# MoE 2 with experts 1 to 7 in falling order of their token counts, and with 480 to 352 rows by place in that order

## The chip, the core and the metric

The kernel runs on one core of a Trainium2 chip. The metric is the device time of one execution in microseconds (us); smaller is better. Its engines are TensorE (PE, with PEld for its weight loads), VectorE (DVE), ScalarE (ACT), GpSimd (POOL) and SyncE (SP). Here SP only issues DMA transfers; POOL issues the indirect ones. Each engine works through its own instructions in a fixed order.

## The reference

A linear-attention layer and a first mixture block ("MoE 1") give `x` with N = 3072 tokens of D = 384. The change concerns what follows, the second mixture ("MoE 2"), where each token goes to the one expert of eight with the largest logit:

```
logits = x @ w_gate                      # 3072 x 8
expert_idx = np.argmax(logits, axis=1)
...
for e in range(E):                       # E = 8, F = 1024
    mask = expert_idx == e
    xe = x[mask]
    h = np.maximum(xe @ w1[e], 0.0)      # 384 -> 1024
    ye = h @ w2[e]                       # 1024 -> 384
    out[mask] = gate_w[mask, None] * ye
```

So the work per expert depends on how many tokens chose it, which is known only when the last token has been routed. Worked out from the reference's own inputs, expert 0 has 426 tokens, and experts 1 to 7 have, sorted, 469, 416, 410, 390, 361, 322 and 278.

## The kernel before

Attention fills about the first half of the time; MoE 1 then runs over six blocks of 512 tokens, from about 550 to 846 us. After each block `route` finds every token's expert and its rank within it, and POOL scatters the token's row (384 values, its gate weight, its number) into the DRAM table `slots`, which has 512 places (`CAP`) for each expert. A token beyond place 512 is left to a loop at the end (`For_i`, line 1519), which runs no turn when every count is at most 512.

MoE 2 takes expert after expert, 0 to 7, always with all 512 places, filled or not. Products keep float32 accuracy by splitting each operand into a high and a low part (H, L), so each product is three matmuls. `load_expert` issues four weight DMAs of 768 KB on SP into buffers `r` (pool `wr`, four buffers) and then makes the split weights: ACT copies the high part (line 249: six of 128x512 into `a1H`, eight of 128x384 into `a2H`), and POOL subtracts for the low part (line 250). Two pools, `wwa` and `wwb`, hold split weights of alternate experts. `load_rows` loads an expert's rows from `slots` in tiles of 128 (line 1199), `load_xt` transposes them on PE (`pxe`, line 1208) and splits them with ACT and DVE (`yTH`, `yTL`, lines 1209 and 1210).

`unit` computes one expert. For each of eight slices f of the 1024 hidden values, the first layer is nine matmuls into `ph` (line 1234; the moving operand is the rows, so its columns are the rows' number). ACT and DVE make `hH` and `hL` of it (1237, 1238). The second layer (lines 1222 to 1224, `pz`) is three matmuls for each tile of up to 128 rows: there the rows are the stationary operand, and the 384 columns of the weights move. The second layer of slice f runs behind the first layer of slice f + 1. At the end of a unit the next expert's transposes go in front of the last slice's second layer; then ACT scales each tile (`yo`, 1254) and POOL scatters it to the output (1255).

Expert 0 is done in two halves: its first 256 rows run (`half1`) while the last block is still being routed, with `gH`, `gL` in place of `hH`, `hL`, in pools of MoE 1; the other 256 rows follow in `expert_pass`. Buffers of `expert_pass` lie where MoE 1's buffers were, so its first row load waits for the last readers of those. The order of instructions on each engine is decided when the kernel is built. Before `expert_pass`, PE sums the counts (`pcn`, line 1474), DVE forms the number of extra turns `nx_`, and SP reads it into a register (line 1516).

Of the kernel before, what the change touches and what calls it, by code (L numbers as in the profile page):

```python
# [7 lines left out]
FP32 = mybir.dt.float32  # L8
# [3 lines left out]
I32 = mybir.dt.int32  # L12
# [168 lines left out]
def kernel(ctx: ExitStack, tc: tile.TileContext, q, k, v, beta, w_in, w_out, w_gate, w1, w2, out):  # L181
# [977 lines left out]
    def bank(name):  # L1159
        return ps.tile([128, 512], FP32, tag="ps", name=name)  # L1160

    wr = ahead["wr"]
    wwa = ctx.enter_context(tc.tile_pool(name="wwa", bufs=1, reuse_waits="tile"))

# [7 lines left out]

    def load_expert(e, wpool):
        r1, r2 = [], []
        for x in range(2):
            t_ = wr.tile([128, KD, F2 // 2], FP32, tag="rst", name="r1")
            load(e, out=t_, in_=w1[e].rearrange("(c p) f -> p c f", p=128)[:, :, x * F2 // 2:(x + 1) * F2 // 2])
            r1.append(t_)
        for x in range(2):
            t_ = wr.tile([128, KF2 // 2, DM], FP32, tag="rst", name="r2")  # L1180
            load(e, out=t_, in_=w2[e].rearrange("(c p) f -> p c f", p=128)[:, x * KF2 // 2:(x + 1) * KF2 // 2])
# [12 lines left out]

    def load_rows(e, sl, tiles, rpool, tag, bufs=2):
        rw = []
        for t in tiles:
            r_ = rpool.tile([128, RW], FP32, tag=tag, name="rw", bufs=bufs)
            last_rows[:] = [nc.sync.dma_start(out=r_, in_=sl[e * CAP + t * 128:e * CAP + (t + 1) * 128]).ins]
            rw.append(r_)  # L1200
        return rw

    def load_xt(rw, xt):
        n = len(rw) * 128
        for c in range(KD):
            p_ = bank("pxe")[:, 0:n]
            for t, r_ in enumerate(rw):
                pe.transpose(p_[:, t * 128:(t + 1) * 128], r_[:, c * 128:(c + 1) * 128], ident)
            act.activation(xt[0][:, c, 0:n], p_, ACTF.Copy)
            dve.tensor_tensor(xt[1][:, c, 0:n], p_, xt[0][:, c, 0:n].bitcast(FP32), ALU.subtract)  # L1210
        return xt

    def unit(ws, rw, xt, hpool, tags, ytag, between=None, final=False):

        a1, a2 = ws
        n, nt = 128 * len(rw), len(rw)
        py = [bank(f"pz{t}") for t in range(nt)]

        def second(fp, hh, hl, t):
            ts_ = slice(t * 128, (t + 1) * 128)  # L1220
# [31 lines left out]
        for t in range(nt):  # L1252
            yo = ytag[0].tile([128, 512], FP32, tag=ytag[1], name="yo", bufs=ytag[2])[:, 0:DM]
# [13 lines left out]

    pre = load_expert(0, wwa)
    with mx:
# [16 lines left out]
        eb = wp.tile([128, E], FP32, name="eb")  # L1286
        dve.tensor_copy(eb, ebi)
        tidi = wp.tile([128, 4], I32, name="tidi")
        for hb in range(2):
# [125 lines left out]
        for b in range(NT // 512):  # L1415
# [7 lines left out]
            for f in range(NF2 + SK):  # L1423
# [31 lines left out]
                if b == NT // 512 - 1:  # L1455
                    if f == SK + 1:
                        pad_first()
                    if f == SK + 4:
                        first["rows"] = load_rows(0, slots, range(2), rp, "row2")
                    if f == NF2 - 1:  # L1460
                        first["xt"] = load_xt(first["rows"], x_tiles(b + 1))
# [4 lines left out]
        step(last, 1)  # L1466
        half1 = unit(step(pre, 99), first["rows"], first["xt"], gp, ("gH", "gL", SK + 1), (gp, "t", 2))
        step(half1, 3)
        step(last, 1)
        step(half1, 2)  # L1470

        pk = bank("pcn")
        for n, x in enumerate(counts):
            pe.matmul(pk[:, 0:E], oneb, x, start=n == 0, stop=n == len(counts) - 1)
        mc = const.tile([128, 1], FP32, name="mc")
        dve.tensor_reduce(mc, pk[:, 0:E], AX.X, ALU.max)
        mci = const.tile([128, 1], I32, name="mci")
        dve.tensor_scalar(mci, mc, -1.0, None, ALU.add)
        nx_ = const.tile([128, 1], I32, name="nx_")
# [4 lines left out]
    wwb = ctx.enter_context(tc.tile_pool(name="wwb", bufs=1, reuse_waits="tile"))  # L1484
    hp = ctx.enter_context(tc.tile_pool(name="hp", bufs=3, reuse_waits="tile"))
# [4 lines left out]

    def expert_pass(sl, ws, t0):

        rw = load_rows(0, sl, range(t0, CAP // 128), yp, "rw", 8)
        xt = load_xt(rw, new_xt())
        for e in range(E):
            nx = load_expert(e + 1, (wwb, wwa)[e % 2]) if e + 1 < E else None
            nxt = []
            if nx:
                step(nx, 1)
                nrw = load_rows(e + 1, sl, range(CAP // 128), yp, "rw", 8)  # L1500
            run = unit(ws, rw, xt, hp, ("hH", "hL", 3), (yp, "yo", 4), (lambda: nxt.extend(load_xt(nrw, new_xt()))) if nx else None, final=not nx)
# [7 lines left out]
            if nx:  # L1509
                ws = step(nx, 99)  # L1510
                rw, xt = nrw, nxt

    expert_pass(slots, step(pre, 99), FIRST // 128)


    extra = nc.values_load(nx_[0:1, 0:1], min_val=0, max_val=NT // CAP)
    off = const.tile([128, 1], FP32, name="off")
    dve.memset(off, 0.0)
    with tc.For_i(0, extra, 1):
        dve.tensor_scalar(off, off, float(CAP), None, ALU.add)  # L1520
        clear_slots()
        for i in range(NT // 128):
# [43 lines left out]
```

## Time and profile before

| | |
|---|---|
| median of 3 runs | 1159.25 us (1151.38 to 1160.28) |
| the profiled execution | 1153.81 us, span 1152.1 us |
| busy, whole span | PE 938.5 us (81%), DVE 641.1, ACT 639.1, POOL 451.5 |
| expert 0's first half begins on PE | 846.16 us |
| its second half begins (first transpose) | 869.36 us |
| last second-layer matmul of expert 7 begins | 1136.13 us |

The busy shares are means over stages of different kind; MoE 2 is a stage of its own and is read from its own stretch. On PE consecutive matmuls overlap, so the distance between starts tells what one costs, not its printed duration. "Idle before, releaser" at the end of a timeline row is how long the engine had waited and for what.

### The profile page before, as it was taken

To read this page: it belongs to the slowest core of one execution; us is meant where nothing else is said; L and a number is where in the kernel's file an instruction comes from. 1 tells how busy PE (TensorE), PEld (TensorE's weight loads), DVE (VectorE), ACT (ScalarE), POOL (GpSimd) and SP (SyncE) were. 2 spreads that over 40 slices of the span, in tenths; PEclk is the share of its full clock that TensorE was granted. 3 is DMA by queue.
4 is the path that set the end of the run, shared out by engine and by line. 5 is a ranking of instruction groups with operands and counts; after the bars stand their busy time and mean duration, and the time that the engine had idled before them with its cause. 6 is when DMAs were issued, how large, how long until landed. Compare 5 with 4: busy or idle time off the path is not lost.

```text
span 1152.1 us, 23064 instructions
## 1 busy us (share of the span) xinstructions
PE 938.5 (81%) x9149; PEld 857.7 (74%) x9149; DVE 641.1 (56%) x1548; ACT 639.1 (55%) x1258; POOL 451.5 (39%) x451
## 2 busy tenths in 40 slices
PE   1222687688766788889899999999997999999994
PEld 0212587577656777787789988989896999999994
DVE  6778877978858959664875454444341222221220
ACT  4565899788797796785673333333324344432321
POOL 4453363554444723433432031210115665445611
PEclk9999999798778998889899999999998999999997
DMA  7976487594794975554654123230217543334100
GB/s 179 207 165 112 60 157 143 129 166 90 169 150 112 193 150 134 131 166 153 223 162 139 56 84 104 54 121 1 98 57 251 170 128 116 114 124 143 52 26 25
DMA packets 258727, 144.45 MB, mean 125 GB/s; under 512 B 200221, under 2 KB 241217, under 8 KB 258608
## 3 DMA queue, kind: packets, MB, share of 16 engines
q1 hardware_dynamic: 250480, 124.67, 45.9%
q0 software_dynamic: 7584, 17.41, 4.7%
q8 instruction: 73, 1.20, 0.4%
q10 hardware_dynamic: 544, 0.80, 0.2%
q14 instruction: 46, 0.38, 0.1%
HBM read 77.41 MB, written 36.60 MB: 99 GB/s over the span
## 4 chain that ended last, share of the span: by engine, by line
PE 43%; DVE 21%; issue 14%; ACT 10%; DMA 5%; POOL 4%; SPq 1%; POOLq 0%; ACTq 0%; DVEq 0%
PE ph L1234 9%; PE ph L1436 7%; DVE sub L35 3%; DVE Xp L35 3%; PE pz L1222 3%; PE pz L1224 3%; PE pz L1223 3%; PE ph L35 3%; DVE nw L35 3%; PE py L35 2%; PE py L1451 2%; PE py L1452 2%; PE py L1450 2%; ACT W L35 2%; DVE uL L35 1%
## 5 line engine op out<-in xcount | busy, mean ns | idle before, releaser
L1238 DVE SCALAR_TENSOR_TENSOR hL<-ph,hH 128x512 fp32r<-128x512 f32 (+1 forms) x64 | 42.0, 658 | 191.9 <-ACT hH L1237 191.9
L1237 ACT ACTIVATE hH<-ph 128x512 fp32r<-128x512 f32 (+1 forms) x64 | 36.8, 577 | 132.7 <-PE ph L1234 132.6
L1439 ACT ACTIVATE t<-ph,half 128x512 f32<-128x512 f32 x66 | 45.4, 688 | 93.7 <-PE ph L1436 93.2
L1440 DVE SCALAR_TENSOR_TENSOR t<-t,ph 128x512 f32<-128x512 f32 x66 | 45.2, 686 | 87.2 <-ACT t L1439 87.0
L1255 POOL DMA_INDIRECT out_dram<-yo,rw x32 | 31.3, 977 | 134.8 <-ACT yo L1254 129.9
L1222 PE MATMUL pz<-a2H,hH 128*128 128x384 f32 x240 | 81.9, 341 | 2.5 <-ACT hH L1237 2.5
L35 POOL TENSOR_TENSOR Pst<-pm,Pst 64x512 f16<-64x512 f32 x48 | 56.4, 1175 | 64.1 <-ACT Pst L35 63.0
L1224 PE MATMUL pz<-a2H,hL 128*128 128x384 f32 x240 | 81.4, 339 | 0.0
L1223 PE MATMUL pz<-a2L,hH 128*128 128x384 f32 x240 | 81.0, 338 | 0.0
L1396 POOL DMA_INDIRECT slots<-row,di x24 | 23.9, 997 | 144.7 <-DVE di L1388 139.2
L35 POOL TENSOR_TENSOR gL<-t,gH 128x256 fp32r<-128x256 f32 x60 | 46.5, 775 | 85.5 <-ACT gH L35 82.5
L1444 DVE TENSOR_TENSOR gL<-t,gH 128x512 fp32r<-128x512 f32 x66 | 54.6, 827 | 39.6 <-ACT gH L1443 38.8
L1234 PE MATMUL ph<-yTH,a1L 128*128 128x512 f32 (+1 forms) x192 | 73.5, 383 | 0.0
L1234 PE MATMUL ph<-yTL,a1H 128*128 128x512 f32 (+1 forms) x192 | 73.4, 382 | 0.0
L1234 PE MATMUL ph<-yTH,a1H 128*128 128x512 f32 (+1 forms) x192 | 72.7, 380 | 0.0
L35 PE MATMUL ph<-xTH,wiH 128*128 128x256 f32 x180 | 59.5, 330 | 12.6 <-DVE t L35 7.8
L1443 ACT ACTIVATE gH<-t 128x512 fp32r<-128x512 f32 x66 | 41.6, 631 | 47.7 <-DVE t L1440 47.7
L1450 PE MATMUL py<-woH,gH 128*128 128x392 f32 x192 | 65.6, 342 | 0.8 <-ACT gH L1443 0.8
L1451 PE MATMUL py<-woL,gH 128*128 128x392 f32 x192 | 65.3, 340 | 0.0
L1452 PE MATMUL py<-woH,gL 128*128 128x392 f32 x192 | 65.3, 340 | 0.0
L35 DVE TENSOR_TENSOR Xp<-Xp,sub 128x31 f32<-128x31 f32 (+15 forms) x186 | 63.7, 343 | 2.6
L35 DVE TENSOR_TENSOR sub<-Bt,Xp 128x31 f32<-128x31 f32 (+15 forms) x186 | 61.7, 332 | 4.9 <-POOL Bt L35 1.5
(306 smaller groups left out, 3261.0 us busy)
## 6 DMA issues: line engine op xcount, KB each, us to landing
r<-in_moe_w_dram SPq DMA_DIRECT2D x32, 768.0 KB, 4.5
slots<-zrow SPq DMA_DIRECT2D x8, 784.0 KB, 5.6
rw<-slots SPq DMA_DIRECT2D x32, 196.0 KB, 2.5
stage<-in_moe_w_in_dram SPq DMA_DIRECT2D x16, 384.0 KB, 3.7
stage<-in_moe_w_out_dram SPq DMA_DIRECT2D x16, 384.0 KB, 3.9
row<-ypart SPq DMA_DIRECT2D x6, 784.0 KB, 4.5
ysave<-row SPq DMA_DIRECT2D x6, 784.0 KB, 3.6
kr<-in_k_dram SPq DMA_DIRECT2D x24, 192.0 KB, 4.7
```

Of the source, the lines that this page charges most:

```text
L35: return self.fn(*self.a, **self.k)
L1222: pe.matmul(o, hh[:, ts_], a2[0][:, fp], start=fp == 0, stop=False)
L1223: pe.matmul(o, hh[:, ts_], a2[1][:, fp], start=False, stop=False)
L1224: pe.matmul(o, hl[:, ts_], a2[0][:, fp], start=False, stop=fp == KF2 - 1)
L1234: pe.matmul(ph, a1[a][:, c, fs], xt[x][:, c, 0:n], start=k == 0, stop=k == 3 * KD - 1)
L1436: pe.matmul(ph, wi(a, f)[:, c], xt[x][:, c], start=n == 0, stop=n == 3 * KD - 1)
L1439: act.activation(t_, ph, ACTF.Relu, bias=half, scale=1.0 / 6.0)
L1440: dve.scalar_tensor_tensor(t_, t_, 1.0, ph, ALU.min, ALU.mult)
L1444: dve.tensor_tensor(gL, t_, gH.bitcast(FP32), ALU.subtract)
L1450: pe.matmul(o, gh[:, ts_], wo(0, fp), start=fp == 0, stop=False)
L1451: pe.matmul(o, gh[:, ts_], wo(1, fp), start=False, stop=False)
L1452: pe.matmul(o, gl[:, ts_], wo(0, fp), start=False, stop=fp == NF2 - 1)
```

## The change

Experts 1 to 7 are taken in falling order of their counts. Place p of that order has a fixed number of rows `ROWS[p]`; expert 0 stays first with 512. DVE ranks the seven counts by comparing each pair and writes the expert's number for each place into `places`; SP reads one number per place into a register, and weights and rows of that place are loaded from an address that the register gives. The weights of place 1 are now issued before the rows of expert 0's second half. Tiles need not have 128 rows: 480 rows are three tiles of 128 and one of 96. If a count is above its place's rows, `more` is 1 and the loop at the end does everything again with 512 rows (its first turn now starts at offset 0).

```diff
+    ROWS = [512, 480, 448, 416, 400, 384, 384, 352]
...
-    def load_expert(e, wpool):
+    def load_expert(e, wpool, place=None):
+        s1, s2 = (w1[e], w2[e]) if place is None else [x[bass.ds(place, 1)].rearrange("o r f -> (o r) f") for x in (w1, w2)]
...
+        yield
+        wpool = pools[wpool]
...
-    def load_rows(e, sl, tiles, rpool, tag, bufs=2):
+    def load_rows(e, sl, lo, hi, rpool, tag, bufs=2, place=None):
+        src = ... sl.rearrange("(e r) w -> e r w", r=CAP)[bass.ds(place, 1)].rearrange("o r w -> (o r) w")
+        for t in range(lo, hi, 128):
+            n = min(128, hi - t)
...
-                pe.transpose(p_[:, t * 128:(t + 1) * 128], r_[:, c * 128:(c + 1) * 128], ident)
+                pe.transpose(p_[:, t * 128:t * 128 + m], r_[:, c * 128:(c + 1) * 128], ident[0:m, 0:m])
...
-        n, nt = 128 * len(rw), len(rw)
+        hs, nt = height(rw), len(rw)
+        n = sum(hs)
...
+        dve.tensor_copy(ck, pk[:, 0:E])
+        dve.scalar_tensor_tensor(key, ck[:, 1:E], float(E), rev[:, 1:E], ALU.mult, ALU.add)
+        dve.tensor_tensor(above, ...key..., ...key..., ALU.is_gt)
+        dve.tensor_reduce(place, above, AX.X, ALU.add)
+        dve.tensor_tensor(at, ...place..., ...placef..., ALU.is_equal)
+        dve.tensor_tensor(above, at, ...placef..., ALU.mult)
+        dve.tensor_reduce(key, above, AX.X, ALU.add)
+        dve.tensor_copy(places[:, 1:E], key)
+        number = {1: who(1)}
+        pre = load_expert(1, "b", number[1])
+        step(pre, 1)
+        dve.tensor_tensor(over[:, 1:E], key, rowsf[:, 1:E], ALU.is_gt)
+        dve.tensor_reduce(more, over, AX.X, ALU.max)
+        dve.tensor_scalar(nx_, nx_, 1.0, more, ALU.add, ALU.mult)
...
-        rw = load_rows(0, sl, range(t0, CAP // 128), yp, "rw", 8)
+        rw = load_rows(0, sl, t0, rows[0], yp, "rw", 8)
...
+            if nx is None and e + 1 < E:
+                    number[e + 1] = who(e + 1)
```

The change moves instructions in three places. The first is SP between expert 0's halves: `r` are the weights of the next expert, the first `rw` rows those of expert 0's second half, and ISA forms an address from the register. Before:

```order
L1516 TENSOR_LOAD nx__12471
L1516 ISA x2
L1199 DMA rw<-slots 128x392 x2
L1168 DMA r_12604<-in_moe_w_dram 128x3x512
L1168 DMA r_12606<-in_moe_w_dram 128x3x512
L1168 DMA r_12608<-in_moe_w_dram 128x4x384
L1168 DMA r_12610<-in_moe_w_dram 128x4x384
L1199 DMA rw<-slots 128x392 x4
```

After:

```order
L1515 TENSOR_LOAD places
L1170 ISA
L1170 DMA r_12499<-in_moe_w_dram 128x3x512
L1170 ISA
L1170 DMA r_12501<-in_moe_w_dram 128x3x512
L1170 ISA
L1170 DMA r_12503<-in_moe_w_dram 128x4x384
L1170 ISA
L1170 DMA r_12505<-in_moe_w_dram 128x4x384
L1210 DMA rw<-slots 128x392 x2
```

The four weight loads stand in front of the two row loads now, and behind a register load that needs the ranking instead of `nx_`.

The second place is ACT from the last two slices of expert 0's first half (`gH`) to the start of its second half (`yTH`, `hH`). Before:

```order
L1237 ACTIVATE gH<-ph_12513 128x256
L1237 ACTIVATE gH<-ph_12533 128x256
L1254 ACTIVATE yo<-pz_12335,rw 128x384
L1254 ACTIVATE yo<-pz_12336,rw 128x384
L1209 ACTIVATE yTH<-pxe 128x256 x3
L249 ACTIVATE a1H<-r_12604 128x512 x3
L1237 ACTIVATE hH<-ph_12634 128x256
L1237 ACTIVATE hH<-ph_12652 128x256
L249 ACTIVATE a1H<-r_12606 128x512 x3
L1237 ACTIVATE hH<-ph_12676 128x256
```

After:

```order
L1253 ACTIVATE gH<-ph_12561 128x256
L250 ACTIVATE a1H<-r_12499 128x512 x3
L1253 ACTIVATE gH<-ph_12581 128x256
L250 ACTIVATE a1H<-r_12501 128x512
L1270 ACTIVATE yo<-pz_12351,rw 128x384
L1270 ACTIVATE yo<-pz_12352,rw 128x384
L250 ACTIVATE a1H<-r_12501 128x512 x2
L250 ACTIVATE a2H<-r_12503 128x384 x4
L250 ACTIVATE a2H<-r_12505 128x384 x4
L1224 ACTIVATE yTH<-pxe 128x256 x3
L1253 ACTIVATE hH<-ph_12672 128x256
```

All fourteen weight copies moved from the second half's slices to places ahead of `yTH`, and three of them ahead of the first half's last `gH`.

The third place is PE where place 4 (400 rows, `pz_13828` to `pz_13831`) hands over to place 5 (384 rows). Before, at each expert's end, there stood

```order
L1208 MATMUL pxe<-ident,rw 128x128 x12
```

and four tiles of 128 rows. Now the last tile of place 4 has 16 rows, and place 5 has nine transposes:

```order
L1238 MATMUL pz_13831<-a2H,hH 16x384
L1239 MATMUL pz_13831<-a2L,hH 16x384
L1240 MATMUL pz_13831<-a2H,hL 16x384
L1223 MATMUL pxe<-ident,rw 128x128 x9
L1238 MATMUL pz_13828<-a2H,hH 128x384
```

A short tile keeps its three matmuls of 384 columns in each slice; only places 5, 6 and 7, with 384, 384 and 352 rows, have a tile less.

## Rows read from the trace of the kernel before

**Rows 1.** Stretches of 20 and 40 us: window, its length, busy us of PE, PEld, DVE, ACT, POOL, clock, DMA share, GB/s
```profile
960.00:1000.00 40.00, 40.00 (x215) 36.57 (x214) 9.42 (x15) 19.56 (x41) 20.48 (x20) 1.00 0.37 112
560.00:580.00 20.00, 18.43 (x105) 16.49 (x103) 19.96 (x40) 13.53 (x28) 8.72 (x10) 1.00 0.44 138
```
**Rows 2.** Who PE waited for from 840 us on: total us, times, longest
```profile
PE pxe L1208 <- DMA rw<-slots: 5.4, 1, 5.4
PE pz L1222 <- ACT hH L1237: 2.5, 1, 2.5
```
**Rows 3.** Chain that ended last, one expert of 512 rows: start us, us, what
```profile
970.16 2.08 PE ph L1234 x9
...
974.34 2.08 PE ph L1234 x9
```
**Rows 4.** Timeline of PE where one expert of 512 rows follows another: start us, us, what
```profile
960.37 1.47 PE L1208 MATMUL pxe<-ident,rw 128*128 128x128 f32 x12
961.60 0.42 PE L1222 MATMUL pz<-a2H,hH 128*128 128x384 f32 x1
```
**Rows 5.** Timeline of PE, expert 0's first half, 256 rows
```profile
858.47 0.28 PE L1234 MATMUL ph<-xH,a1H 128*128 128x256 f32 x1
...
859.54 0.34 PE L1222 MATMUL pz<-a2H,gH 128*128 128x384 f32 x1
...
860.60 0.28 PE L1234 MATMUL ph<-xH,a1H 128*128 128x256 f32 x1
```
**Rows 6.** Timeline of PE between expert 0's two halves, and early in the second
```profile
863.57 0.34 PE L1224 MATMUL pz<-a2H,gL 128*128 128x384 f32 x1
869.36 1.80 PE L1208 MATMUL pxe<-ident,rw 128*128 128x128 f32 x6 [5.45 <-DMA rw<-slots]
...
876.76 0.69 PE L1222 MATMUL pz<-a2H,hH 128*128 128x384 f32 x1 [2.54 <-ACT hH L1237]
...
878.84 0.42 PE L1234 MATMUL ph<-yTH,a1H 128*128 128x256 f32 x1
```
**Rows 7.** Timeline of SP's DMA queue in the same place
```profile
866.93 0.83 SPq L1199 DMA_DIRECT2D rw<-slots  x2
867.81 2.27 SPq L1168 DMA_DIRECT2D r<-in_moe_w_dram  x4
```
**Rows 8.** Line 1516, the register load: duration ns min/median/max, first and last start
```profile
L1516 SPq TENSOR_LOAD <-nx__12471 x1: 478/478/478, 854.9 to 854.9; - x1
L1516 SPq FUSED_REGOPS  x1: 192/192/192, 855.5 to 855.5; - x1
```
**Rows 9.** Timeline of ACT in the same place
```profile
861.87 0.39 ACT L1237 ACTIVATE gH<-ph 128x256 fp32r<-128x256 f32 x1 [1.75 <-PE ph L1234]
863.42 1.10 ACT L1254 ACTIVATE yo<-pz,rw 128x384 f32<-128x384 f32 x2 [1.18 <-PE pz L1224]
870.55 1.02 ACT L1209 ACTIVATE yTH<-pxe 128x256 fp32r<-128x256 f32 x3 [6.03 <-PE pxe L1208]
874.77 1.67 ACT L249 ACTIVATE a1H<-r 128x512 fp32r<-128x512 f32 x3 [3.19 <-DMA r<-in_moe_w_dram]
```
**Rows 10.** Timeline of DVE at the count of the tokens
```profile
854.35 0.17 DVE L1476 TENSOR_REDUCE mc<-pcn 128x1 f32<-128x8 f32 x1 [0.24 <-PE pcn L1474]
854.55 0.15 DVE L1478 TENSOR_SCALAR mci<-mc 128x1 int32<-128x1 f32 x1
```
**Rows 11.** Timeline of POOL, the splits of one expert's weights
```profile
968.50 7.57 POOL L250 TENSOR_TENSOR a1L<-r,a1H 128x512 fp32r<-128x512 f32 x6
976.01 7.80 POOL L250 TENSOR_TENSOR a2L<-r,a2H 128x384 fp32r<-128x384 f32 x8
```
**Rows 12.** Line 1168, the weight loads: time from issue to landing
```profile
DMA to landing us min/median/max: 4.3/4.5/11.5
```
**Rows 13.** Two stretches of 3 us between and in expert 0's halves, columns as Rows 1
```profile
866.00:869.00 3.00, 0.00 (x0) 0.00 (x0) 0.00 (x0) 0.00 (x0) 0.53 (x1) 0.50 0.63 199
875.00:878.00 3.00, 1.24 (x4) 1.25 (x5) 0.76 (x2) 3.00 (x8) 2.52 (x3) 0.70 1.04 385
```

More of the change, by code (lines that the diff above doesn't have):

```diff
@@ L1162 @@
     wr = ahead["wr"]
+    late = ctx.enter_context(tc.tile_pool(name="late", bufs=1))
     wwa = ctx.enter_context(tc.tile_pool(name="wwa", bufs=1, reuse_waits="tile"))
@@ L1215, in unit @@
         a1, a2 = ws
-        n, nt = 128 * len(rw), len(rw)
-        py = [bank(f"pz{t}") for t in range(nt)]
+        hs, nt = height(rw), len(rw)
+        n = sum(hs)
+        py = [bank(f"pz{t}")[0:m] for t, m in enumerate(hs)]
         def second(fp, hh, hl, t):
-            ts_ = slice(t * 128, (t + 1) * 128)
+            ts_ = slice(t * 128, t * 128 + hs[t])
             o = py[t][:, 0:DM]
@@ L1252, in unit @@
         for t in range(nt):
-            yo = ytag[0].tile([128, 512], FP32, tag=ytag[1], name="yo", bufs=ytag[2])[:, 0:DM]
+            yo = ytag[0].tile([128, 512], FP32, tag=ytag[1], name="yo", bufs=ytag[2])[0:hs[t], 0:DM]
             act.activation(yo, py[t][:, 0:DM], ACTF.Copy, scale=rw[t][:, DM:DM + 1])
@@ L1287 @@
         dve.tensor_copy(eb, ebi)
+        places = late.tile([128, E], I32, name="places")
+        pool.iota(out=places, pattern=[[1, E]], base=0, channel_multiplier=0)
+        placef = late.tile([128, E], FP32, name="placef")
+        dve.tensor_copy(placef, places)
+        rowsf = late.tile([128, E], FP32, name="rowsf")
+        for e, n in enumerate(ROWS):
+            dve.memset(rowsf[:, e:e + 1], float(n))
         tidi = wp.tile([128, 4], I32, name="tidi")
@@ L1458 @@
                     if f == SK + 4:
-                        first["rows"] = load_rows(0, slots, range(2), rp, "row2")
+                        first["rows"] = load_rows(0, slots, 0, FIRST, rp, "row2")
                     if f == NF2 - 1:
@@ L1466 @@
         step(last, 1)
-        half1 = unit(step(pre, 99), first["rows"], first["xt"], gp, ("gH", "gL", SK + 1), (gp, "t", 2))
+        first["ws"] = step(pre, 99)
+        half1 = unit(first["ws"], first["rows"], first["xt"], gp, ("gH", "gL", SK + 1), (gp, "t", 2))
         step(half1, 3)
@@ L1470, with wide @@
         step(half1, 2)
+        def wide(name, dt=FP32, n=E - 1):
+            return late.tile([128, n, E - 1] if n else [128, E - 1], dt, name=name)
         pk = bank("pcn")
@@ L1474 @@
             pe.matmul(pk[:, 0:E], oneb, x, start=n == 0, stop=n == len(counts) - 1)
-        mc = const.tile([128, 1], FP32, name="mc")
-        dve.tensor_reduce(mc, pk[:, 0:E], AX.X, ALU.max)
-        mci = const.tile([128, 1], I32, name="mci")
+        ck = late.tile([128, E], FP32, name="ck")
+        dve.tensor_copy(ck, pk[:, 0:E])
+        key, above, at, place = wide("key", n=0), wide("above"), wide("at"), wide("place", n=0)
+        dve.scalar_tensor_tensor(key, ck[:, 1:E], float(E), rev[:, 1:E], ALU.mult, ALU.add)
@@ new lines, with who @@
+        dve.tensor_copy(places[:, 1:E], key)
+        def who(e):
+            return nc.values_load(places[0:1, e:e + 1], engines=[mybir.EngineType.SP], min_val=0, max_val=E - 1,
+                                  skip_runtime_bounds_check_because="a sum of one of the numbers 1 to E - 1: the ranks of distinct keys are distinct")
+        number = {1: who(1)}
+        pre = load_expert(1, "b", number[1])
+        step(pre, 1)
+        over, more = late.tile([128, E], FP32, name="over"), late.tile([128, 1], FP32, name="more")
@@ new lines @@
+        dve.tensor_tensor(at, at, ck[:, 1:E].unsqueeze(1).to_broadcast([128, E - 1, E - 1]), ALU.mult)
+        dve.tensor_reduce(key, at, AX.X, ALU.add)
+        dve.tensor_tensor(over[:, 1:E], key, rowsf[:, 1:E], ALU.is_gt)
+        dve.tensor_tensor(over[:, 0:1], ck[:, 0:1], rowsf[:, 0:1], ALU.is_gt)
+        dve.tensor_reduce(more, over, AX.X, ALU.max)
+        mc = late.tile([128, 1], FP32, name="mc")
+        dve.tensor_reduce(mc, ck, AX.X, ALU.max)
+        mci = late.tile([128, 1], I32, name="mci")
@@ L1478 @@
         dve.tensor_scalar(mci, mc, -1.0, None, ALU.add)
[L1479 removed]
+        nx_ = late.tile([128, 1], I32, name="nx_")
         dve.tensor_scalar(nx_, mci, CAP.bit_length() - 1, None, ALU.logical_shift_right)
+        dve.tensor_scalar(nx_, nx_, 1.0, more, ALU.add, ALU.mult)
         step(half1, 99)
[L1484 removed]
+    pools["b"] = ctx.enter_context(tc.tile_pool(name="wwb", bufs=1, reuse_waits="tile"))
@@ L1511, in expert_pass @@
                 rw, xt = nrw, nxt
-    expert_pass(slots, step(pre, 99), FIRST // 128)
+            nx = None
+    expert_pass(slots, first["ws"], FIRST, ROWS, pre, number)
     extra = nc.values_load(nx_[0:1, 0:1], min_val=0, max_val=NT // CAP)
-    off = const.tile([128, 1], FP32, name="off")
-    dve.memset(off, 0.0)
+    off = late.tile([128, 1], FP32, name="off")
+    dve.memset(off, -float(CAP))
     with tc.For_i(0, extra, 1):
```

32 lines of the change are left out of this document (20 added, 12 removed).

## The prediction

> **What bounds the kernel now.** I read the busy shares by stretch first, then the waits of PE, then the chain and PE's timeline. From 960 to 1000 us, more than one whole expert, PE is busy 40.00 of 40 us at full clock, while ACT has 19.56, POOL 20.48 and the DMA engines a share of 0.37 [rows 1]. From 840 us to the end PE waits for others only twice, 5.4 us for expert 0's second rows and 2.5 us for `hH` [rows 2]. So MoE 2 is bound by PE, apart from the seam between expert 0's halves: columns taken from PE are time taken from the end, as long as no other engine takes PE's place.
>
> What does a row cost? In an expert of 512 rows one slice is 4.18 us: nine first-layer matmuls in 2.08, which leaves 2.10 for twelve of the second layer, 0.175 each [rows 3]. In expert 0's first half nine matmuls of 256 columns take 1.07 us, and six of the second layer 1.06 [rows 5]: the first layer goes with the rows, the second with the tiles of 128. Twelve transposes take 1.23 us [rows 4]. An expert is thus 8 x 4.18 + 1.23 = 34.7 us.
>
> **Steady part: what is removed.** Places 1 to 7 drop 32 + 64 + 96 + 112 + 128 + 128 + 160 = 720 rows. First layer: (2.08 - 1.07) / 256 x 8 = 0.0316 us a row and expert [rows 3, 5], so 22.7 us. Second layer: places 1 to 4 keep four tiles, since a tile of 16 rows still has 384 columns moving past it; only places 5 to 7 lose one, 3 tiles x 24 matmuls x 0.175 = 12.6 us. Transposes: nine whole ones at 1.23 / 12 go, 0.9 us; the short ones may save between nothing and 336 rows x 3 / 128 x 0.10 = 0.8 us, and I take 0.4. Sum: 36.6 us (36.2 to 37.0).
>
> The Trainium skill, "TensorE: Matmul & The Clock Gate", section Back-to-back issue gap, gives columns / 2.4 GHz plus 2.5 ns for a matmul in a stream. By it 512 columns would be 0.216 us and 384 columns 0.163, and the two layers would save an estimated 21.6 + 11.7 = 33.3 us against 35.3 by the rows. The trace has 0.231 and 0.175, so the rows decide.
>
> **Do other engines keep up?** The shortest unit with a successor has 384 rows and three tiles: 8 x (9 + 9) x 0.175 + 0.9 = 26.1 us, taking a first-layer matmul of 384 columns as one of the second layer. POOL's splits of one expert are 7.57 + 7.80 us [rows 11], and with its scatters it has 20.48 in 40 us [rows 1], 17.8 an expert; ACT has 17.0 by the same scaling. Both fit. For the register, SP adds per expert one load of 0.48 us and up to eight address steps of 0.19 [rows 8], 2.0 us, on a queue that mostly waits for buffers. These cost nothing while the weights arrive a unit ahead. Where a unit ends, the work of PE that covers ACT's and DVE's `yTH`, `yTL` falls from twelve second-layer matmuls to nine, by 0.5 us, at up to three boundaries: 0 to 2 us of new waits, and I take 0.5.
>
> **The seam: what moves.** Before, SP issued expert 0's second rows at 866.93 and the next weights only behind them, at 867.81 [rows 7]. PE stopped after the matmul at 863.57, transposed at 869.36, and stopped again for 2.54 us until 876.76, since `hH` stood on ACT behind three `a1H` copies whose weights had not landed before 874.77 [rows 6, 9]. Now the weights come first. The ranking is about eight dependent DVE steps where `mc` was; two such steps start 0.20 us apart [rows 10], so `places` is done near 854.35 + 1.6 = 856.0. With 0.48 for the load and 0.19 for the address [rows 8], the first weights are issued near 856.8, eleven us earlier. The wait at 876.76 goes: 2.54 us. With it goes a slow spell: the granted clock, at 0.50 (1.2 GHz) in the first pause, was back at 0.70 on the mean from 875 to 878 [rows 13], and the six second-layer matmuls from 876.76 to 878.84 took 2.08 us where 1.06 is usual [rows 5, 6]. That is 3.5 us in all.
>
> Against it stands the new order on ACT: three `a1H` copies are in front of the last `gH`, which ran at 861.87 [rows 9]. A weight load lands 4.3 us after its issue at best, 4.5 in the median, 11.5 at worst [rows 12]. I take 5.3, a little above the median because three more follow at once: landed at 862.1. The three copies take 1.67 us [rows 9], `gH` runs at 863.8, then `gL` and six matmuls, and `yo`, formerly at 863.42, at 865.1: 1.7 late. The rows of the second half are issued 3.5 us after `yo` [rows 7, 9], as they wait for its scatter, so they and PE's transposes slip by 1.7 as well. They are behind 3.1 MB of weights, but at the 385 GB/s that the DMA reached [rows 13] those need 8.2 us from 856.8 and are through before 868.6, when the rows are issued. The other ten copies ahead of `yTH` take at most 10 x 0.56 = 5.6 us from 866.2 and end by 871.8; `yTH` would be due 1.2 us after the transposes start, at 872.2. So 1.7 us, and the seam gains 3.5 - 1.7 = 1.8. The ends: with weights after 4.3 us, a gain of 2.8; after 11.5 us, `gH` is 8.1 late, `yo` 7.9, and the seam loses 4.4.
>
> **Small additions.** Ten small DVE steps go into the first block of MoE 1, where DVE is busy 19.96 of 20 us and PE 18.43 [rows 1]; at 0.15 us each [rows 10] they are worth 0 to 1.5, I take 0.5. The DVE steps after the count run between `gL` steps while PE has a slice to do. `more` should be 0, and the loop then runs no turn, as before.
>
> **Sum.** -36.6 - 1.8 + 0.5 + 0.5 = -37.4 us. The span of 1152.1 becomes 1114.7, and the profiled execution's 1153.81 us 1116.4. That execution is 5.4 us below the median of the three runs, 1159.25, from which the same step leads to 1121.9. I forecast 1119, between the two.
>
> **Rivals.**
> Late weights (A): the landing is near 11.5 us, because four loads share the queue, ACT stands at `a1H`, and PE's pause at the seam grows. For it: the weights' 6.96 us from issue to copy in rows 7 and 9. Against: two row loads were ahead of them then. Time: 1119 + 1.8 + 4.4 = 1125.
>
> Short tiles are dear (B): a stationary operand of 96, 64, 32 or 16 columns loads more slowly than one of 128, and its load no longer hides. Five short tiles (places 1 to 4 and 7) have 24 matmuls each; if each cost one slot of 0.175 us more, 21.0 us come back: 1140. Against: in rows 5 a load of 128 columns hides behind matmuls 0.119 us apart, and nothing in the trace makes a smaller one longer. The Trainium skill, "TensorE: Matmul & The Clock Gate", section Weight-path perf modes, says the fast weight load is on only for 128 weights of a type other than FP32. If this type has it, short tiles lose it; no run here shows a short tile.
>
> Supply (C): loads by register are issued or land later, and three-tile units wait for weights. POOL's 17.8 us leave 8.3 us of room in 26.1, so it decides only if such a load is over 8 us later. If the three shortest units took 31 us, about 15 us come back: 1134.
>
> The extra turn (D), slower: a count above its place's rows sets `more`, and the loop does all again. That is at least 8 x 34.7 = 278 us, about 1397 or more. It decides at one token: the sorted counts 469, 416, 410, 390, 361, 322, 278 are all below 480, 448, 416, 400, 384, 384, 352, but the third by only 6, and the counts on the chip could differ by close logits.
>
> **How the numbers follow.** The forecast has 0.80, A 0.10, B 0.03, C 0.04, D 0.03. The likeliest case gives 1119. Below, 1151.38, the lowest run, less 37.0 and the seam's 2.8, gives 1111.6, and 1110 allows 2 more; above, the highest run 1160.28 less 36.2, with 4.4, 2.0 and 1.5 lost, gives 1132. The range 1110 to 1131 holds the forecast and A. One per cent, about 11.6 us, is what a measurement can tell from no change: forecast, A, B and C are all faster by more, 0.97 together, of which I give 0.01 to an in-between case within 1%; D is slower.
>
> **What would show it.** In the changed profile, nine `ph` matmuls should take 2.08 - 0.00394 us per row dropped: 1.95 at 480, 1.58 at 384, 1.45 at 352. Twelve second-layer matmuls should still take 2.1 us a slice at places 1 to 4, nine 1.6 at 5 to 7; if short tiles take longer, B. The units should go from about 33.7 us down to 26. The first weight load should be issued near 857, PE's idle time from the first half's last slices to the transposes add up to about 7 us instead of 5.45, and the 2.54 us wait be gone; above 10 us it is A. PE's waits from 900 us on should total under 2 us; waits for `a1H` or `a1L` there are C. A second set of `out` scatters after place 7 is D. The forecast fails if PE isn't what ends last in the shorter units.

## The result and the profile after

The changed kernel takes 1122.84 us (median of four runs, 1122.07 to 1125.64) against 1158.7 us for the kernel before on the same chip: ratio 0.970, 95% interval 0.966 to 0.974. In a second set it took 1121.62 us, ratio 0.967 (0.965 to 0.969). The profiled execution is 1123.02 us with a span of 1121.3. The forecast was 1119 us, with a range of 1110 to 1131.

The stretches after, columns as in [rows 1]: more than one expert at 1.00 clock, and a stretch of the three-tile places.

```profile
960.00:1000.00 40.00, 40.00 (x226) 36.72 (x225) 8.55 (x15) 20.75 (x43) 20.50 (x20) 1.00 0.38 112
1040.00:1060.00 20.00, 20.00 (x121) 19.96 (x120) 4.81 (x10) 9.91 (x23) 12.90 (x14) 1.00 0.58 198
```

PE is still busy in all of both. What it waited for from 840 us on, beside [rows 2]:

```profile
PE pxe L1223 <- DMA rw<-slots: 7.0, 1, 7.0
PE pz L1238 <- ACT gH L1253: 1.2, 1, 1.2
```

The first wait lies between expert 0's halves, the second in the last slice of its first half; none is left at a later place. The chain that ended last, for nine first-layer matmuls at 480, 416 and 384 rows, beside 2.08 in [rows 3]:

```profile
904.84 1.96 PE ph L1250 x9
...
972.27 1.70 PE ph L1250 x9
...
1034.50 1.56 PE ph L1250 x9
```

PE's timeline at three handovers, into place 1 (last tile of 96 rows), 2 (64 rows) and 5 (nine whole tiles), beside [rows 4]. The distance to the row after the transposes is their price.

```profile
896.38 1.40 PE L1223 MATMUL pxe<-ident,rw 128*128 128x128 f32 x12
897.57 0.42 PE L1238 MATMUL pz<-a2H,hH 128*128 128x384 f32 x1
...
928.96 2.05 PE L1223 MATMUL pxe<-ident,rw 128*128 128x128 f32 x12
930.94 0.44 PE L1238 MATMUL pz<-a2H,hH 128*128 128x384 f32 x1
...
1079.04 1.08 PE L1223 MATMUL pxe<-ident,rw 128*128 128x128 f32 x9
1079.89 0.42 PE L1238 MATMUL pz<-a2H,hH 128*128 128x384 f32 x1
```

The seam, on SP, ACT, POOL and PE, in place of [rows 6, 7, 9]:

```profile
862.22 2.41 SPq L1170 DMA_DIRECT2D r<-in_moe_w_dram  x4
...
867.24 1.67 ACT L250 ACTIVATE a1H<-r 128x512 fp32r<-128x512 f32 x3 [1.99 <-DMA r<-in_moe_w_dram]
868.82 0.36 ACT L1253 ACTIVATE gH<-ph 128x256 fp32r<-128x256 f32 x1
869.23 0.44 PE L1238 MATMUL pz<-a2H,gH 128*128 128x384 f32 x1 [1.25 <-ACT gH L1253]
870.42 0.63 ACT L250 ACTIVATE a1H<-r 128x512 fp32r<-128x512 f32 x1 [1.25 <-DMA r<-in_moe_w_dram]
870.96 1.04 ACT L1270 ACTIVATE yo<-pz,rw 128x384 f32<-128x384 f32 x2
...
873.08 0.98 POOL L1271 DMA_INDIRECT out_dram<-yo,rw  x1 [0.30 <-ACT a1H L250]
...
875.17 3.05 SPq L1210 DMA_DIRECT2D rw<-slots  x6
...
877.67 1.62 PE L1223 MATMUL pxe<-ident,rw 128*128 128x128 f32 x6 [7.02 <-DMA rw<-slots]
```

The weights leave early, ACT's copies of them hold back the last `gH` and then `yo`, and PE stops for 1.25 us at `gH` and 7.02 us at the rows, but no longer for `hH`.

**Where the time went.** In this kernel the first matmul of expert 0's first half starts at 851.40, against 846.16 before, and the span ends at 1121.3 against 1152.1. So MoE 2, from that matmul to the end, went from 305.9 to 269.9 us, 36.0 less, while the part ahead of it is 5.2 us longer in this execution. The table, worked out from PE's timelines and the spans, is what the experiments below are read by ("seam": from that first matmul to the second half's transposes, and from there to the transposes of the next expert).

| kernel | first half starts | MoE 2 | seam | median, us |
|---|---|---|---|---|
| before | 846.16 | 305.9 | 23.2 + 22.5 | 1158.7 |
| before again (x1) | 849.20 | 307.8 | 23.3 + 24.3 | |
| changed | 851.40 | 269.9 | 26.3 + 18.7 | 1122.8 |
| changed again (y1) | 849.93 | 270.0 | 25.9 + 18.9 | 1121.6 |
| 512 rows everywhere (x2) | 847.63 | 304.9 | 26.2 + 18.6 | 1156.1 |
| whole tiles (x3) | 849.75 | 279.2 | 25.8 + 18.9 | 1131.9 |
| full transposes (x4) | 850.92 | 268.1 | 26.0 + 18.9 | 1118.3 |
| late weights (y2) | 847.41 | 268.3 | 23.0 + 20.3 | 1119.5 |
| late weights, full transposes (z1) | 847.09 | 268.1 | 23.1 + 22.3 | 1118.8 |
| copies behind `yo` (y3) | 852.73 | 269.8 | 25.8 + 19.0 | 1123.6 |
| rows early (y4) | 848.81 | 267.1 | 17.6 + 26.4 | 1120.4 |
| own `yo` (z2) | 850.96 | 267.7 | 17.5 + 27.2 | 1120.6 |
| rows early, `yo` in place (z3) | 853.82 | 259.0 | 17.6 + 18.6 | 1113.1 |
| the same, expert 0 with 448 (w1) | 848.94 | 263.7 | 17.6 + 23.1 | 1114.5 |

The expectations count the changed kernel's MoE 2 as 269.7: they take its start from the chain, which has 851.57, and not from PE's timeline.

### The profile page after: what moved, and what is told of

Same layout as the page of the kernel before. It is cut to its first block, busy times and chain, and to the rows that moved or that the text cites. A ratio compares the mean times of both kernels' runs of the same rounds, so it can differ in the third digit from the quotient of the medians.

```text
span 1121.3 us, 23042 instructions
## 1 busy us (share of the span) xinstructions
PE 908.4 (81%) x9068; PEld 838.1 (75%) x9068; DVE 638.1 (57%) x1571; ACT 632.2 (56%) x1255; POOL 449.6 (40%) x449
## 4 chain that ended last, share of the span: by engine, by line
PE 51%; DVE 21%; ACT 10%; issue 6%; POOL 4%; DMA 4%; SPq 1%; POOLq 0%; ACTq 0%; DVEq 0%
PE ph L1459 11%; PE ph L1250 7%; PE py L1474 4%; PE py L1473 4%; PE py L1475 4%; DVE sub L35 3%; DVE Xp L35 3%; PE ph L35 3%; PE py L35 3%; PE pz L1238 3%; PE pz L1239 3%; PE pz L1240 3%; DVE uL L35 2%; DVE nw L35 1%; DVE KS L35 1%
## 5 line engine op out<-in xcount | busy, mean ns | idle before, releaser
L1254 DVE SCALAR_TENSOR_TENSOR hL<-ph,hH 128x384 fp32r<-128x384 f32 (+6 forms) x64 | 36.1, 564 | 163.5 <-ACT hH L1253 163.5
L1253 ACT ACTIVATE hH<-ph 128x384 fp32r<-128x384 f32 (+6 forms) x64 | 31.7, 495 | 112.5 <-PE ph L1250 112.5
L1238 PE MATMUL pz<-a2H,hH 128*128 128x384 f32 (+1 forms) x216 | 73.1, 339 | 0.0
L1271 POOL DMA_INDIRECT out_dram<-yo,rw x29 | 28.1, 969 | 111.1 <-ACT yo L1270 106.9
L1239 PE MATMUL pz<-a2L,hH 128*128 128x384 f32 (+1 forms) x216 | 72.4, 335 | 0.0
L1240 PE MATMUL pz<-a2H,hL 128*128 128x384 f32 (+1 forms) x216 | 72.4, 335 | 0.0
L1250 PE MATMUL ph<-yTL,a1H 128*128 128x384 f32 (+6 forms) x192 | 65.7, 342 | 0.0
L1250 PE MATMUL ph<-yTH,a1L 128*128 128x384 f32 (+6 forms) x192 | 65.6, 342 | 0.0
L1250 PE MATMUL ph<-yTH,a1H 128*128 128x384 f32 (+6 forms) x192 | 65.5, 342 | 0.0
```

The lines of the kernel that those rows point to most:

```text
L1250: pe.matmul(ph, a1[a][:, c, fs], xt[x][:, c, 0:n], start=k == 0, stop=k == 3 * KD - 1)
```

## Experiments

### Does the change make the part ahead of MoE 2 longer?

The kernel before, unchanged, profiled again.

> The kernel before, once more, for its profile. Of the 6.6 us that the changed kernel's span lies above the forecast of 1114.7, 5.4 are there before MoE 2: expert 0's first half begins at 851.57 us, against 846.16 in the profile of before, and the shift grows inside attention, where no instruction was moved. Theory 1 (attention's length varies from execution to execution): this profile's first half begins somewhere else than 846.16, by 1 us or more, and from there to the span's end it takes 305.9 us within 0.7. Theory 2 (the change itself makes the part ahead of MoE 2 longer, through new buffers or addresses): it begins within 1 us of 846.16 again, and only kernels with the change begin near 851.6.

Its first half starts at 849.20, 3.0 us later than in the first profile of the same kernel, so attention's length varies and theory 1 holds. MoE 2 took 307.8 us, 1.2 more than its bound allowed; that is the seam, where the wait for `hH` was 3.0 us and the granted clock was 0.50 (1.2 GHz) from 880.48 to 884.48 behind it:

```profile
PE pz L1222 <- ACT hH L1237: 3.0, 1, 3.0
...
880.48:882.48 2.00, 2.00 (x7) 2.00 (x8) 0.46 (x2) 1.50 (x3) 2.00 (x2) 0.50 1.06 379
```

> The changed kernel once more, beside the other kernels of this set. If attention's length varies from execution to execution (as the second profile of before says: first half of expert 0 at 849.2 us instead of 846.2, and 847.6 in the changed kernel with 512 rows at every place), its first half begins somewhere between 846 and 853 us; from there to the span's end it takes 269.7 us within 1. If the change itself makes the part ahead longer, it begins at 851.5 within 1 again. Median 1122.8 within 2.

The changed kernel again has 849.93 and 270.0. Over the twelve profiles with the change the start lies between 847.1 and 853.8, on the mean 849.9. For the kernel before, the median of 1158.7 less the 1.7 us around the span and the 305.9 to 307.8 of MoE 2 gives 849.2 to 851.1. So the first profile of before was one with a short attention, and no shift ahead of MoE 2 can be seen.

### The rows and the tiles

All 512, with ranking, register loads and early weights kept:

```diff
-    ROWS = [512, 480, 448, 416, 400, 384, 384, 352]
+    ROWS = [512] * 8
```

> The changed kernel with 512 rows at every place: ranking, register loads and the early weights stay, only the cut of rows and tiles is undone. Theory 1 (the gain is the rows and tiles that PE no longer does; ordering and the seam are worth little): the first layer and second layer come back with 22.7 + 12.6 us, nine whole transposes with 0.9, while the short tiles' transposes, which take 1.8 us more than whole ones in the changed kernel, get cheaper by that: +34.4 us, so 304.1 us from expert 0's first half to the span's end (269.7 in the changed kernel, 305.9 before) and about 1157 us. Theory 2 (the early weights and the new order bring more than the 1.8 us forecast): clearly below 300 us for that part, and below 1152 us.

This kernel took 304.9 us in MoE 2 and 1156.07 us, ratio to before 0.9975 (0.9955 to 0.9995). The cut of rows and tiles is 304.9 - 269.9 = 35.0 of the 36.0 us; all the rest, ordering and early weights, is 1.0 to 2.9 by the two profiles of before. Theory 1 holds.

Next, each place's rows rounded up to whole tiles:

```diff
-    ROWS = [512, 480, 448, 416, 400, 384, 384, 352]
+    ROWS = [512, 512, 512, 512, 512, 384, 384, 384]
```

> The changed kernel with each place's rows rounded up to whole tiles: 512 at places 1 to 4, 384 at 5 to 7. Theory 1 (the first layer pays by the row, the second by the tile, and short transposes are dear): 336 rows x 0.0316 = 10.6 us come back, and 1.8 us of dear transposes go: +8.8 us, 278.5 us from expert 0's first half to the end, about 1131.6 us. Rival B of the prediction (a short stationary tile is dear in the second layer): five short tiles x 24 matmuls x 0.175 = 21 us go, so that the time falls by about 10 us instead, to 1113.

It took 279.2 us and 1131.88 us (ratio 0.977, 0.973 to 0.980), against 278.5 and 1131.6 of theory 1. Rival B is out: a short tile is no dearer in the second layer. But short transposes are dearer than whole ones, which the next kernel takes alone. It loads and transposes 128 rows of each tile, and uses only the place's rows behind that:

```diff
-            last_rows[:] = [nc.sync.dma_start(out=r_[0:n], in_=src[t:t + n]).ins]
-            rw.append(r_[0:n])
+            last_rows[:] = [nc.sync.dma_start(out=r_, in_=src[t:t + 128]).ins]
+            rw.append((r_, n))
...
-                pe.transpose(p_[:, t * 128:t * 128 + m], r_[:, c * 128:(c + 1) * 128], ident[0:m, 0:m])
+                pe.transpose(p_[:, t * 128:(t + 1) * 128], r_[:, c * 128:(c + 1) * 128], ident)
```

> The changed kernel, but every tile of rows is loaded and transposed with all 128 rows, whatever the place's number; the layers and the copies behind the transposes still use only the place's rows. Theory 1 (a transpose of a tile of 64, 32 or 16 rows is dearer than one of 128): the twelve transposes at the three boundaries into places 2, 3 and 4 take 1.23 us again instead of 1.89, 1.81 and 1.76, so 267.9 us from expert 0's first half to the end instead of 269.7, and about 1121.0 us. Theory 2 (the extra time at these boundaries is not the height but a wait that the trace hides, for rows that land late or for a bank): the three groups still take about 1.8 us, 269.7 us and 1122.8 us.

It took 268.1 us in MoE 2, 1.8 less, and 1118.28 us (ratio 0.964, 0.961 to 0.967). The handover that took 1.98 us (928.96 to 930.94) now takes 1.23:

```profile
928.39 1.47 PE L1222 MATMUL pxe<-ident,rw 128*128 128x128 f32 x12
929.62 0.42 PE L1239 MATMUL pz<-a2H,hH 128*128 128x384 f32 x1
```

Theory 1 holds: it is the height, and transposing all 128 rows is faster than transposing 64. In the changed kernel the weight loads show where the time lies (timeline of PEld at the same handover):

```profile
928.79 0.42 PEld L1223 LDWEIGHTS pxe<-ident,rw 128*128 128x128 f32 x3
929.38 0.51 PEld L1223 LDWEIGHTS pxe<-ident,rw 64*128 64x128 f32 x4 [0.17 <-issue]
930.06 0.52 PEld L1223 LDWEIGHTS pxe<-ident,rw 64*128 64x128 f32 x4 [0.17 <-issue]
930.74 0.14 PEld L1223 LDWEIGHTS pxe<-ident,rw 64*128 64x128 f32 x1 [0.17 <-issue]
```

Ahead of each 64-row load the loads pause for 0.17 us, where they otherwise run on under the matmuls; a wait for rows that land late would not come back at each of the three. With a 96-row tile there is no such pause, and twelve take 1.19. The Trainium skill, "TensorEngine Tiling (Array Packing)", section Key Properties, says that a change of the array's tiling mode drains TensorE, and its section Available Configurations lists modes with 128, 64 and 32 rows. The pauses at 64, 32 and 16 rows, and none at 96, agree with it. That it is the mode was not tested by itself.

### The seam: when the weights are issued

The early weights undone:

```diff
-        number = {1: who(1)}
-        pre = load_expert(1, "b", number[1])
-        step(pre, 1)
+        number = {}
...
-    expert_pass(slots, first["ws"], FIRST, ROWS, pre, number)
+    expert_pass(slots, first["ws"], FIRST, ROWS, None, number)
```

> The changed kernel with the one move in the seam undone: the weights of place 1 are issued behind the rows of expert 0's second half again, as before; ranking and register loads stay. Theory 1 (the early weights take away the wait for hH in the second half, but give most of it back, since three weight copies on ACT now stand ahead of the last gH, and one more ahead of yo): 23.2 us from the first half's start to the second half's first transpose (26.2 in the changed kernel), then 22.5 to 24.3 us to the transposes of the next expert (18.7 in the changed kernel, 22.5 and 24.3 in the two profiles of before): 270 to 272.4 us from expert 0's first half to the end, 1123 to 1125.5 us. Theory 2 (the longer pause comes from something else of the change, the ranking or the register load ahead of the rows): the first of the two stays near 26 us, and the whole near 274 us.

The pause is back at 5.4 us, as theory 1 has it, but behind it only 20.3 us pass: MoE 2 takes 268.3 us, 1.6 less than with early weights, where 270 to 272.4 was expected (the whole kernel: 1119.52 us, ratio 0.967, 0.964 to 0.969). The wait for `hH` was only 1.5 us, and the clock (columns as in [rows 1]) stayed at full speed behind it:

```profile
876.45:878.45 2.00, 1.50 (x9) 1.50 (x10) 0.75 (x2) 2.00 (x6) 2.00 (x3) 1.00 1.06 379
```

Whether that is the rule or one landing was tried with the same seam in a kernel that also transposes whole tiles:

> The changed kernel with two edits that each took about 1.6 us from MoE 2 so far: the weights of place 1 issued behind expert 0's second rows (268.3 us from expert 0's first half to the end in place of 269.8), and whole tiles transposed (268.1). Theory 1 (the two lie at different places and add up): 266.6 us, and about 1118 us at the median start of MoE 2. It is also a second look at the seam with late weights: if the gain there is that the wait for hH is short enough that the granted clock does not fall again, the wait is below 2 us and no stretch behind it is below 1.00. Theory 2 (the seam with late weights only had a lucky landing): a wait of 2.5 to 3 us, a second fall of the clock behind it as in both profiles of before, and 268 to 270 us.

Theory 2 holds for the clock and the time, though the wait was only 1.9 us: the clock fell again, and the two gains did not add up (268.1 us; 1118.81 us, ratio 0.967).

```profile
876.00:878.00 2.00, 0.98 (x4) 0.98 (x5) 0.76 (x2) 2.00 (x6) 2.00 (x2) 0.88 1.06 376
878.00:880.00 2.00, 2.00 (x10) 2.00 (x9) 0.00 (x0) 0.80 (x2) 2.00 (x3) 0.50 1.06 373
```

So with late weights the seam takes 43.4 to 47.6 us over four profiles (two of the kernel before), 45.5 on the mean, by when one load lands and whether the clock falls a second time; with early ones 44.7 to 45.0 in six, 44.8 on the mean. By these means the early weights are worth about 0.7 us, less than the spread of the late ones, and by the medians of whole runs no gain shows (1121.6 us early, 1119.5 late, in the same set). What they bring is that the second stop is gone.

Why do they not bring more? Here ACT's copies stand behind `yo`, by an ordering edge from the last `yo` of the first half to each copy:

```diff
-        act.activation(dst[0], src_ap, ACTF.Copy)
+        a = act.activation(dst[0], src_ap, ACTF.Copy)
+        if last_yo:
+            tc.add_manual_dep(a.ins, last_yo[0].name,
+                              mybir.DependencyInfo(mybir.DependencyClass.NoSync, mybir.DependencyReason.DATA), reason="program order")
...
-            act.activation(yo, py[t][:, 0:DM], ACTF.Copy, scale=rw[t][:, DM:DM + 1])
+            y = act.activation(yo, py[t][:, 0:DM], ACTF.Copy, scale=rw[t][:, DM:DM + 1])
+            if hpool is gp:
+                last_yo[:] = [y.ins]
```

> The changed kernel with the early weights kept, but ACT's copies of these weights put behind the two yo of expert 0's first half. Theory 1 (ACT's queue is what makes the pause longer): the last gH comes 1.6 us earlier and yo 2.8 us earlier, with them the scatters, the issue of the second half's rows and the transposes; the copies run while ACT waits for these. 23.4 us instead of 26.2 from the first half's start to the transposes, 18.7 us from there on as in the changed kernel: 266.9 us from expert 0's first half to the end and about 1120 us. Theory 2 (the weights' 3.1 MB on the DMA queues are what delays the rows): gH and yo come earlier, but the rows land as late as now: 269.7 us and 1122.8 us. Theory 3 (the copies are then late for the transposes' own copies yTH): the pause gets shorter, but 2 to 3 us of waits for yTH or hH come behind it.

Theory 2 holds, against the explanation of the prediction: `gH` and `yo` run early again, and the total doesn't move (269.8 us; 1123.62 us, ratio 0.968). Here are POOL, SP and two stretches of 2 us (DMA share second to last):

```profile
871.99 0.97 POOL L1277 DMA_INDIRECT out_dram<-yo,rw  x1 [0.30 <-ACT a1H L250]
...
876.10 3.05 SPq L1214 DMA_DIRECT2D rw<-slots  x6
...
872.00:874.00 2.00, 0.00 (x0) 0.00 (x0) 0.00 (x0) 2.00 (x5) 1.99 (x2) 0.79 1.08 384
874.00:876.00 2.00, 0.00 (x0) 0.00 (x0) 0.00 (x0) 2.00 (x6) 2.00 (x3) 0.50 0.35 135
```

The rows wait until the scatters have read `yo`. From the second scatter to the rows' issue it is 1.38 us before (865.55 to 866.93), 2.09 in the changed kernel, and 4.11 here. The 3.1 MB of weights were issued from 863.55 on, the DMA engines are full until about 874, and only then, at 875.57 by the chain, is the scatter through. Taking ACT out of the way only let the scatters stand longer behind the weights.

### The seam: what waits for the scatters

The rows of the second half into a buffer of their own (with whole transposes and the copies behind `yo`):

```diff
-        rw = load_rows(0, sl, t0, rows[0], yp, "rw", 8)
+        rw = load_rows(0, sl, t0, rows[0], rpool or yp, "rw", 2 if rpool else 8)
```

with `late` passed as `rpool` for the pass that follows the first half.

> Three edits on the changed kernel: transposes of whole tiles (as in the set before), ACT's copies behind yo, and the two row tiles of expert 0's second half in a buffer of their own, so that their loads wait for no reader of MoE 1's buffers and are issued ahead of the weights. Theory 1 (the pause between the halves is only the way from yo over its scatter to the buffer, the row load and the transposes): the transposes follow the first half's last matmuls with less than 2 us of waiting, so beside the 1.7 us of the transposes and the 2.8 us of the copies some 5 us more go: 260 us from expert 0's first half to the end, about 1113 us. Theory 2 (the split rows yTH and yTL wait for the same buffers): the transposes come early, but the first layer behind them waits for yTH until the scatters are through, and only the row load's 2 to 3 us are gained: 263 us, about 1116 us.

Theory 2 holds for the place of the wait, but MoE 2 takes 267.1 us instead of 263 (1120.39 us, ratio 0.967). The transposes follow the first half at once, and then the split rows wait, since their buffers too lie where the scatters still read:

```profile
874.48 0.94 ACT L1228 ACTIVATE yTH<-pxe 128x256 fp32r<-128x256 f32 x3 [2.59 <-DMA out_dram<-yo,rw]
...
874.92 0.80 PE L1255 MATMUL ph<-yTH,a1H 128*128 128x256 f32 x2 [7.66 <-ACT yTH L1228]
```

The other way, on the late weights with whole transposes: only `yo` in a buffer of its own.

```diff
-    half1 = unit(..., ("gH", "gL", SK + 1), (gp, "t", 2))
+    half1 = unit(..., ("gH", "gL", SK + 1), (late, "yo", 2))
```

> The kernel of the run before, with yo of expert 0's first half in a buffer of its own, so that the loads of the second half's rows need not wait until the scatters have read MoE 1's buffers. Theory 1 (between the halves PE waits for that scatter, and for the weights' traffic only where it stands ahead of it): the rows are issued right behind the first half's last matmuls, about 3 us earlier, and the pause of 5.4 us becomes 2.5 to 3: about 263.6 us from expert 0's first half to the end, 1115 us. Theory 2 (the split rows yTH and yTL wait for the same scatters): the transposes come early, but the first layer waits for yTH, and the whole stays at 266 to 267 us.

The rows came early (PE waited 1.9 us for them), and `yTL` waited for a scatter until 7.8 us after the second one had been issued at 870.23, again with weights (from 869.33) on the queues. Theory 2 holds, with 267.7 us and 1120.55 us, ratio 0.968. Which buffer it was, the trace doesn't say; the scatter also reads the tokens' numbers from the first half's rows.

```profile
878.02 1.09 DVE L1225 TENSOR_TENSOR yTL<-pxe,yTH 128x256 fp32r<-128x256 f32 x3 [10.65 <-DMA out_dram<-yo,rw]
...
878.50 0.58 PE L1251 MATMUL ph<-yTL,a1H 128*128 128x256 f32 x1 [6.21 <-DVE yTL L1225]
```

Now both at once: the kernel y4 with `yo` written over the rows, which have been transposed by then, and the copies behind `yTH` (`last_xt` is its last copy).

```diff
-            yo = ytag[0].tile(...)[0:hs[t], 0:DM]
+            yo = rw[t][:, 0:DM] if hpool is gp else ytag[0].tile(...)[0:hs[t], 0:DM]
...
+        if number is not None:
+            last_yo[:] = last_xt
```

> The kernel with the rows of the second half in their own buffer and ahead of the early weights (267.1 us from expert 0's first half to the end; there the transposes followed at once, but yTH waited for the scatters of yo, which took 6 us behind the weights' traffic), with two edits: yo of the first half is written over the rows it belongs to, so that no buffer of MoE 2's split rows waits for its scatters, and ACT's copies of the weights stand behind yTH. Theory 1 (with that, nothing in the seam waits for the scatters any more): yTH runs 1 us behind the transposes, PE waits less than 2 us, and 7 to 8 us go: 259 to 260 us, and about 1111 us. Theory 2 (other buffers, hH or the next rows, wait for the same transfers): the 7.7 us wait moves from yTH to hH, and the time stays at 266 to 267 us.

Theory 1 holds: MoE 2 takes 259.0 us, as worked out, and the kernel 1113.08 us where about 1111 was expected, ratio 0.961 (0.960 to 0.963). This is the fastest kernel of the study, 45 us below the one before. PE's two waits from 835 us on, and a stretch of the seam (columns as in [rows 1]):

```profile
PE ph L1256 <- ACT yTH L1229: 0.3, 1, 0.3
PE pz L1244 <- ACT hH L1259: 0.3, 1, 0.3
...
876.00:878.00 2.00, 1.73 (x13) 1.41 (x11) 0.42 (x1) 1.88 (x4) 2.00 (x3) 1.00 1.05 391
```

The clock stays at 1.00 through the whole seam. What the early weights have in this was not tested: there is no run of this kernel with late ones.

### The price of a row below 256 columns

```diff
-    ROWS = [512, 480, 448, 416, 400, 384, 384, 352]
+    ROWS = [448, 480, 448, 416, 400, 384, 384, 352]
```

> The fastest kernel of the sets before (rows of the second half early, yo in place, copies behind yTH; 259.0 us from expert 0's first half to the end, 1113.1 us), with 448 rows instead of 512 for expert 0, which has 426 tokens: one size changed, so that the second half has 192 columns in place of 256. Theory 1 (the price of 0.0316 us a row and expert, read between 256 and 512 columns, holds below 256 too): 64 rows x 0.0316 = 2.0 us, so 257.0 us and about 1111 us; nine first-layer matmuls take 1.07 - 64 x 0.0039 = 0.82 us. Theory 2 (below 256 columns a matmul of this type gets no cheaper, or its weight load no longer hides): 1.07 us or more for nine, and 259 us or more.

The result lies between the two: nine matmuls of 192 columns take 0.98 us (0.109 each), not 0.82 and not 1.07, so a slice gains 0.09 and expert 0 some 0.7 us, not 2.0. The chain shows the late load and a slice, the list of PE's waits the stop:

```profile
864.95 11.22 DMA r<-in_moe_w_dram
...
879.54 0.98 PE ph L1256 x9
...
PE pz L1244 <- ACT hH L1259: 3.1, 1, 3.1
```

The time is no better (263.7 us; 1114.52 us, ratio 0.964, 0.961 to 0.966), because in this profile a weight load took 11.2 us and ACT's copies held `hH` back: PE waited 3.1 us, and the nine matmuls behind that took 0.215 us each, twice as long, at a granted clock of 0.50 (1.2 GHz, from 874 to 878). How often that happens isn't known. The Trainium skill, "TensorE: Matmul & The Clock Gate", section Back-to-back issue gap, gives columns / 2.4 + 2.5 ns as the gap of a single matmul at full clock, and says itself that this counts too little when the columns are few; the prediction took it for the gap in a stream. By it 192 columns would take an estimated 82.5 ns and nine matmuls 0.74 us; the trace has 0.98, so the trace decides.

## Why the prediction was right, and where it was not

The range and the sign held, and MoE 2 shrank by 36.0 us where 37.9 were forecast for it (the 37.4 of the sum without the 0.5 of MoE 1).

- **First layer: right.** The slices are 1.96, 1.84, 1.70, 1.62, 1.56, 1.56 and, at 352 columns, 9 x 0.161 = 1.45 us. Against 2.08 that is 8 x 2.87 = 23.0 us; forecast 22.7.
- **Second layer: right.** Tiles of 96 to 16 rows cost what whole ones cost; in the three-tile places a slice is 3.12 us (1034.50 to 1037.62), 1.56 for nine matmuls where twelve took 2.10: 3 x 8 x 0.54 = 13.0 us, forecast 12.6.
- **Transposes: wrong, by 2.3 us.** The forecast was -0.9 for nine whole ones and -0.4 for the short ones. The seven handovers took 1.19 + 1.98 + 1.90 + 1.86 + 0.90 + 0.90 + 0.85 = 9.6 us against 7 x 1.23 = 8.6. The bounds "between nothing and 0.8" left out that a short one could cost more; I had looked for that only in the second layer (B), where the short side is the stationary columns. In the transposes it is the partitions. A transpose of 64, 32 or 16 rows costs about (1.98 - 0.92) / 3 = 0.35 us, (1.90 - 0.92) / 3 = 0.33 and 0.31, one of 96 rows 0.09, a whole one 0.10.
- **The seam: about the right size, from two terms that were off.** The forecast was -1.8; the seam measured 45.0 against 45.7 and 47.6, so -0.7 to -2.6. PE's idle time up to the transposes is 1.25 + 7.02 = 8.3 us, between the 7 forecast and the 10 from which it would have been A. The wait at 876.76 and the slow spell behind it went, as said: 18.7 against 22.5, so 3.8 us where 3.5 were forecast. (The 0.70 of [rows 13] is not a clock on its way back, as the prediction reads it, but the mean over a second fall: it was 1.00 from 874 to 876, 0.56 from 876 to 878 and 0.59 from 878 to 880.) Against them the pause lost 3.1 us (26.3 against 23.2), not 1.7. The weights were issued 10.8 us after the first half's start (10.6 forecast) and landed 5.0 us later (5.3), and `gH` was 1.7 late. The step that failed is "1.7 late" carried through to the rows: `yo` was 2.3 late, since one more copy stood ahead of it, whose weights came 8 us after the first issue, and the rows 3.0, since the scatters took longer and SP then waited 0.4 us for ACT's `a2H`. And y3 shows that ACT's order isn't the cause I took it for: without it the scatters wait for the weights instead, and the pause is as long.
- **Boundaries: 0 instead of 0.5.** PE waits nowhere behind the seam. Rivals C and D didn't come.
- **The base: too low.** I chose 1119, between 1116.4 from the profiled execution and 1121.9 from the median. That execution had a short attention, as x1 shows, so the median was the right base: with it the same sum, 1121.9, is 0.9 us below what was measured. By the medians the reduction is 35.9 us against the sum's 37.4. That it comes so near is in part luck, since errors of opposite sign meet in it: transposes and seam gave less than forecast, the layers and the boundaries more.

## What to carry to other kernels

Count what a smaller tile does in each use of it: here columns that move past were paid one by one from 512 down to 256, a stationary side was paid per tile, and fewer partitions even cost more, so that padding a transpose to 128 rows was faster. A load that is issued early is not yet early for everyone: ask which small transfers behind it somebody waits for (here a scatter that must leave a buffer before the next rows can come), and take that wait away first. And base a forecast on the median of the runs, not on one profiled execution, when a stage ahead of the change varies.

## What was not expected of the hardware

- Three transposes of 64 rows among nine of 128 made the group 1.98 us long instead of 1.23, with pauses of 0.17 us in the weight loads; 96 rows cost nothing extra. A stationary operand of 96, 64, 32 or 16 columns made no difference at 0.175 us a matmul.
- Two scatters of 192 KB each let the next step go 1.4 us after the second one's start when no weights were under way (before), 4.1 us after it with 3.1 MB of weights issued ahead of them, at a DMA share of 1.08 (y3), and 7.8 us after it with the weights issued around them, at 1.02 to 1.05 (z2).
- A matmul of 192 columns took 0.109 us, one of 256 columns 0.119: a third of what the price between 256 and 512 columns had promised (w1).
